# State-space convolution plus gated MLP on one core: squared lag powers on ScalarE, shared first statistics, a new order of work

## The chip, the cores and the metric

The kernel runs on one core of a Trainium2 chip. The core has a matrix engine (TensorE, PE), a vector engine (VectorE, DVE), an engine for activation functions that can also copy, scale and square (ScalarE, ACT), a general engine (GpSimd, POOL), and an engine that issues most of the DMAs (SyncE, SP). Each engine works through its own list of instructions strictly in order; semaphores hold an instruction back until its inputs are there. The metric is the device time of one execution in microseconds (us), lower is better. The kernel before takes 250.21 us, the median of six runs between 249.08 and 250.87 us.

## The reference

One input, `A_u` (2048 positions, 512 channels, bf16), is normalised over its channels and goes through two branches; their sum and the input itself are the output.

```python
def _layernorm(x, axis=-1, eps=1e-5):
    m = jnp.mean(x, axis=axis, keepdims=True)
    v = jnp.var(x, axis=axis, keepdims=True)
    return (x - m) / jnp.sqrt(v + eps)

# branch A: a long convolution whose kernel is a sum of 128 complex modes per channel
dt = exp(log_dt);  logdA = dt * A;  dB = dt * B
P = exp(logdA[:, :, None] * l)                  # powers for l = 0 .. 2047
K = einsum("dn,dnl,dn->dl", C, P, dB).real      # 512 x 2048 kernel
y = irfft(rfft(xn padded) * rfft(K padded))[:L] + xn * Dskip

# branch B: a gated MLP, 512 -> 1792 -> 512
h = sigmoid(xn @ w_gate) * (xn @ w_up)
out = x + y + h @ w_down
```

## The kernel before, in words

**Branch B** is cut into four groups of 512 positions and 14 slices of 128 hidden columns: 56 units. A unit is a gate product on PE (line 977), a sigmoid on ACT (line 986), an up product on PE (line 992) and a product of the two on DVE (line 1007). The up product lies in PSUM. For the units listed in `UEV`, ACT first copies it to `us_sb` in SBUF (line 1003) and DVE reads it there; for the others DVE reads PSUM directly. The units are numbered 14 times the group plus the slice. Four down products per group follow (line 1025).

**Layer norm.** For each of the 16 tiles of 128 positions DVE takes statistics (`bn_stats` and `bn_aggr`, lines 529 and 530) into `mv` (mean and variance). `ln_small` makes the inverse deviation from them: for the first four tiles with small DVE steps (lines 483 to 492) and one power on GpSimd (line 491), for the others with GpSimd, ACT and DVE. The normalised first four tiles are transposed on PE (line 552) and copied out by ACT (line 557); only then can the first gate product start. The others are transposed by DMA.

**Branch A** has these steps.

- A ladder of eleven squarings makes the powers 1, 2, 4, ... 2048 of each mode's complex factor in fp32 (ACT line 650 squares, DVE lines 656 and 658 finish, ACT line 644 casts to bf16 into `W`).
- The powers for all lags are split in two factors. For each of four blocks of 128 channels (c0 to c3) a table `G` of 16 powers and a table `H` of 41 powers are built. `LAG0` lists the lag of each row of `H`. Eight rows of `H` are plain copies of ladder powers (ACT, line 751), row 0 is one, and 32 rows are complex products of an earlier row with a ladder power. `cmul` makes up to 8 such rows at once with four DVE instructions: two of 256 elements per row (lines 710 and 711, `f_a`), and two of 128 elements per row that combine the halves (lines 715 and 716, `f_b`). A complex number lies as two real and two imaginary values side by side.
- PE contracts `G` and `H` over the modes (line 774, 64 matmuls twice per block), ACT copies out (780), PE rearranges (796), ACT copies out (803). `H` is one buffer: the next block's rows wait for these matmuls.
- The spectra: the input transform runs on PE (673) with ACT copies (675) and a trip through DRAM. For each half of the channels (p0, p1) and eight frequency groups (u0 to u7) come PE (847), ACT (852), DMAs, the kernel spectrum on PE (865) and ACT (867), the product on DVE (871 and 875), PE (888), ACT (892) and a store. p0 needs blocks c0 and c1, p1 needs c2 and c3. Final matmuls (945, 947) and adds on DVE (960, 1042) close the work.

**The order** is written out by hand. `_Plan.add` numbers every piece of work as it is added, and the list `ORDER` gives the sequence in which all pieces are issued; each engine's list is that sequence with the other engines' entries left out. The planner's costs (the numbers in `pl.add`) do not act at run time. Entries 0 to 24 are loads; entry 25 is 14 matmuls on zeros whose result is not used (`keep_warm`, line 515), and 26 to 28 are two such matmuls each.

Of the kernel before, what the change touches and what calls it, by code (L numbers as in the profile page):

```python
# [20 lines left out]
D = 512  # L21
# [152 lines left out]
def _consts():  # L174
# [30 lines left out]
UEV = (2, 3, 7, 8, 11, 14, 16, 17, 18, 19, 20, 21, 22, 23, 24, 25, 26, 27, 28, 29, 30, 31, 32, 33, 34, 35, 36, 37, 38, 39, 40, 41, 44, 54, 55)  # L205
ORDER = [
    0, 30, 1, 4, 39, 29, 32, 31, 33, 49, 2, 3, 40, 41, 51, 34, 11, 12, 7, 6, 5, 53, 43, 50, 10, 14, 52, 35, 36, 37, 42, 44,
    54, 45, 46, 47, 22, 15, 38, 56, 48, 27, 614, 55, 615, 138, 28, 616, 59, 637, 95, 96, 141, 677, 60, 638, 678, 93, 682,
    61, 683, 9, 17, 139, 626, 19, 620, 106, 108, 627, 628, 109, 94, 16, 8, 62, 64, 120, 57, 13, 642, 621, 622, 63, 643, 667,
    659, 657, 20, 23, 18, 97, 142, 668, 672, 658, 98, 660, 662, 132, 632, 65, 673, 66, 633, 663, 634, 635, 623, 684, 58, 99,  # L210
    624, 67, 119, 685, 661, 68, 669, 102, 69, 121, 625, 686, 670, 671, 70, 647, 664, 101, 100, 181, 648, 665, 617, 666, 107,
    71, 103, 618, 619, 652, 639, 26, 649, 73, 122, 653, 72, 124, 640, 75, 111, 650, 123, 74, 641, 182, 183, 184, 651, 636,
    76, 629, 674, 135, 644, 675, 645, 24, 140, 143, 104, 125, 133, 224, 630, 225, 77, 226, 676, 79, 185, 679, 654, 25, 136,
    105, 78, 80, 646, 227, 228, 81, 655, 680, 82, 656, 147, 681, 631, 134, 129, 186, 705, 710, 83, 85, 110, 148, 84, 706,
    86, 177, 687, 150, 688, 229, 187, 88, 137, 708, 703, 87, 151, 149, 689, 89, 704, 188, 753, 152, 709, 178, 91, 740, 153,
    690, 128, 192, 711, 191, 127, 126, 695, 154, 230, 189, 712, 741, 194, 193, 168, 765, 199, 171, 112, 113, 696, 179, 155,
    169, 190, 130, 170, 90, 116, 196, 733, 195, 697, 174, 172, 200, 707, 201, 202, 173, 766, 175, 176, 203, 763, 165, 204,
    754, 734, 205, 206, 209, 210, 207, 114, 197, 713, 714, 758, 723, 156, 166, 764, 208, 724, 738, 213, 131, 167, 157, 759,
    92, 739, 760, 214, 159, 158, 211, 212, 215, 216, 767, 160, 198, 742, 231, 735, 745, 144, 736, 145, 115, 737, 232, 217,
    761, 146, 746, 219, 234, 762, 235, 743, 725, 718, 242, 237, 220, 236, 243, 117, 744, 244, 162, 245, 726, 246, 21, 161,  # L220
    727, 747, 247, 258, 118, 768, 748, 163, 769, 719, 749, 267, 259, 268, 770, 730, 269, 771, 164, 772, 239, 218, 720, 750,
    221, 248, 751, 721, 414, 384, 799, 752, 722, 728, 222, 800, 241, 729, 755, 250, 756, 251, 731, 804, 715, 757, 698, 238,
    716, 270, 271, 415, 223, 831, 732, 717, 805, 385, 354, 773, 416, 774, 249, 252, 240, 386, 801, 233, 699, 253, 420, 418,
    256, 353, 257, 254, 255, 272, 775, 421, 355, 260, 802, 356, 262, 261, 273, 263, 277, 358, 274, 360, 361, 419, 417, 388,
    776, 357, 359, 391, 390, 275, 285, 286, 849, 264, 278, 287, 288, 279, 283, 280, 265, 389, 387, 781, 266, 832, 422, 282,
    782, 423, 281, 829, 783, 392, 301, 289, 302, 830, 850, 393, 777, 290, 424, 425, 803, 291, 293, 394, 376, 362, 369, 691,
    276, 395, 294, 851, 839, 363, 310, 833, 784, 406, 852, 840, 399, 370, 292, 426, 364, 789, 365, 809, 371, 427, 284, 810,
    311, 295, 396, 844, 296, 397, 875, 372, 374, 297, 312, 436, 373, 444, 845, 400, 401, 377, 819, 790, 375, 313, 298, 403,
    407, 846, 378, 379, 299, 300, 380, 314, 408, 876, 847, 848, 445, 366, 820, 446, 405, 398, 428, 404, 367, 791, 824, 303,
    305, 304, 825, 792, 806, 437, 306, 402, 320, 321, 322, 315, 853, 807, 448, 324, 438, 429, 368, 841, 834, 316, 409, 793,  # L230
    328, 447, 451, 430, 880, 842, 323, 835, 431, 410, 329, 330, 808, 452, 411, 453, 449, 843, 331, 332, 459, 450, 466, 412,
    821, 822, 811, 460, 812, 333, 454, 455, 381, 814, 461, 327, 881, 813, 382, 344, 823, 435, 432, 434, 815, 325, 816, 836,
    467, 794, 433, 481, 837, 413, 463, 464, 439, 345, 334, 474, 465, 462, 456, 440, 856, 511, 383, 504, 468, 795, 817, 475,
    826, 335, 818, 338, 838, 469, 476, 827, 326, 457, 480, 828, 470, 854, 441, 442, 857, 855, 317, 858, 339, 877, 307, 505,
    878, 308, 506, 796, 319, 797, 785, 458, 489, 309, 937, 798, 318, 336, 471, 887, 938, 888, 490, 337, 342, 895, 859, 882,
    491, 509, 510, 340, 343, 341, 346, 879, 883, 472, 443, 507, 496, 479, 348, 347, 508, 493, 473, 349, 884, 885, 350, 860,
    477, 494, 478, 492, 495, 351, 352, 610, 604, 598, 861, 862, 482, 483, 945, 512, 484, 513, 485, 867, 497, 498, 486, 487,
# [858 lines left out]
```

## Time and profile before

| what | value |
|---|---|
| median of six runs | 250.21 us (249.08 to 250.87) |
| the profiled execution, its own time | 249.7 us |
| its span (first to last instruction) | 247.9 us |
| PE busy | 221.7 us, 89% |
| DVE busy | 199.5 us, 80% |
| ACT busy | 174.0 us, 70% |
| POOL busy | 15.4 us, 6% |
| first sigmoid starts (line 986) | 16.15 us |
| contraction for c0 / c1 / c2 / c3 starts (line 774) | 81.22 / 108.29 / 139.21 / 172.46 us |
| last compute instruction (line 1042) | 244.66 us, lasting 0.42 us |

The profile comes from one execution; about 1.8 us of its time lie outside its span. The four starts of line 774 cut the execution into stages, and busy time is best read stage by stage: a share over the whole span mixes stretches in which different engines are full. An instruction's duration is also longer than what it takes out of its engine's time, because the next one may start before it ends; so where a price is wanted, the distance from one start to the next is read.

### The profile page before, as it was taken

Reading aid. Unit: us, or ns where it says so; the run is one execution under the profiler, and the core shown is the slowest. Engines: PE = TensorE matmul, PEld = TensorE weight load, DVE = VectorE, ACT = ScalarE, POOL = GpSimd, SP = SyncE. Lnnn points to the kernel's source line nnn. Section 1 sums busy time; section 2 is a strip of 40 time slices with the busy share of each in tenths; the row PEclk is TensorE's granted clock in tenths of the full one; section 3 lists DMA queues with packets and bytes.
Section 4 is the critical chain, followed back from the end, with each engine's and each line's share of the span. In section 5 each row is a group of like instructions: output and inputs, shape, how many; then the busy total and the mean of one; then the engine's idle time right before and its main releaser. Section 6 shows DMA issues by size and latency. Waiting matters only on the chain.

```text
span 247.9 us, 5737 instructions
## 1 busy us (share of the span) xinstructions
PE 221.7 (89%) x2246; PEld 119.6 (48%) x2276; DVE 199.5 (80%) x413; ACT 174.0 (70%) x279; POOL 15.4 (6%) x34
## 2 busy tenths in 40 slices
PE   0199899999989998999899999998999998899993
PEld 0155334444433643455455655444665564445761
DVE  3999899999999999999999999999153244673472
ACT  3599999999999987547497899783447897530000
POOL 2202005000000000103000010000010001000000
PEclk9999999999999999999999999999999999999999
DMA  6999933511437472727835786747668479777333
GB/s 151 235 313 379 351 100 106 148 42 59 155 114 182 135 210 85 187 82 169 204 109 151 197 227 165 211 118 197 187 179 262 119 209 260 194 218 248 127 130 127
DMA packets 50861, 43.64 MB, mean 176 GB/s; under 512 B 12561, under 2 KB 44050, under 8 KB 50834
## 3 DMA queue, kind: packets, MB, share of 16 engines
q1 hardware_dynamic: 48738, 40.58, 55.8%
q0 software_dynamic: 864, 1.57, 4.0%
q10 hardware_dynamic: 1232, 1.11, 1.5%
q8 instruction: 18, 0.29, 0.5%
q14 instruction: 9, 0.07, 0.1%
HBM read 24.64 MB, written 12.06 MB: 148 GB/s over the span
## 4 chain that ended last, share of the span: by engine, by line
DVE 48%; PE 31%; ACT 6%; DMA 5%; SPq 5%; issue 3%; DVEq 0%; ACTq 0%
PE bank L1025 11%; DVE big L710 9%; DVE big L711 9%; DVE hT_sb L1007 6%; DVE big L715 5%; DVE big L716 5%; PE bank L977 5%; SPq L412 5%; PE pair L865 4%; DMA big<-c_E 3%; DVE big L871 3%; PE bank L992 2%; DVE big L658 2%; PE pair L945 2%; DVE stats L529 2%
## 5 line engine op out<-in xcount | busy, mean ns | idle before, releaser
L977 PE MATMUL bank<-xnT,wg_sb 128*128 128x512 bf16 (+1 forms) x225 | 55.3, 373 | 4.3 <-ACT hT_sb L986 1.7
L992 PE MATMUL bank<-xnT,wu_sb 128*128 128x512 bf16 x214 | 53.6, 379 | 1.8 <-DVE hT_sb L1007 0.5
L1025 PE MATMUL bank<-wd_sb,hT_sb 128*128 128x512 bf16 x216 | 50.4, 379 | 0.4
L871 DVE TENSOR_TENSOR big<-big 128x2048 bf16<-128x2048 bf16 x16 | 19.5, 1218 | 20.7 <-ACT big L867 19.8
L977 PEld LDWEIGHTS <-wg_sb 128*128 128x128 bf16 x236 | 22.3, 99 | 28.4 <-issue 7.8
L986 ACT ACTIVATE hT_sb<-bank 128x512 bf16<-128x512 f32 x56 | 33.5, 624 | 3.0 <-PE bank L977 3.0
L992 PEld LDWEIGHTS <-wu_sb 128*128 128x128 bf16 x224 | 20.9, 97 | 27.4 <-issue 5.3
L710 DVE TENSOR_TENSOR big<-big 128x256 bf16<-128x256 bf16 (+5 forms) x52 | 33.0, 635 | 1.0
L1025 PEld LDWEIGHTS <-hT_sb 128*128 128x128 bf16 x224 | 21.5, 98 | 25.1 <-DVE hT_sb L1007 0.4
L711 DVE TENSOR_TENSOR big<-big 128x256 bf16<-128x256 bf16 (+5 forms) x52 | 32.9, 633 | 0.0
L1003 ACT ACTIVATE us_sb<-bank 128x512 bf16<-128x512 f32 x35 | 21.1, 606 | 4.1 <-DVE hT_sb L1007 2.5
L867 ACT ACTIVATE big<-pair 128x1024 bf16<-128x1024 f32 x16 | 16.4, 1028 | 9.9 <-PE pair L865 8.9
L715 DVE TENSOR_TENSOR big<-big 128x128 bf16<-128x128 bf16 (+5 forms) x52 | 21.9, 422 | 1.0
L716 DVE TENSOR_TENSOR big<-big 128x128 bf16<-128x128 bf16 (+5 forms) x52 | 21.6, 415 | 0.0
L852 ACT ACTIVATE big<-pair 128x1024 bf16<-128x1024 f32 x16 | 16.6, 1035 | 6.1 <-PE pair L847 6.1
L865 PE MATMUL pair<-big 128*128 128x256 bf16 x160 | 19.6, 273 | 0.7 <-DMA big<-c_E 0.7
L892 ACT ACTIVATE big<-pair 128x1024 bf16<-128x1024 f32 x16 | 16.3, 1030 | 3.2 <-DMA v_scr<-big 2.1
L865 PEld LDWEIGHTS <-big 128*128 128x128 bf16 x160 | 15.4, 98 | 5.5 <-DMA big<-c_E 1.2
L675 ACT ACTIVATE big<-pair 128x1024 bf16<-128x1024 f32 x16 | 17.1, 1067 | 0.0
L1007 DVE TENSOR_TENSOR hT_sb<-hT_sb,bank 128x512 bf16<-128x512 bf16 x21 | 13.9, 678 | 2.4 <-PE bank L992 1.5
L888 PE MATMUL pair<-big 64*64 64x256 bf16 x384 | 13.7, 272 | 1.1 <-DVE big L871 1.1
L1007 DVE TENSOR_TENSOR hT_sb<-hT_sb,us_sb 128x512 bf16<-128x512 bf16 x35 | 14.1, 415 | 0.0
(95 smaller groups left out, 252.4 us busy)
## 6 DMA issues: line engine op xcount, KB each, us to landing
big<-c_E SPq DMA_DIRECT2D x16, 320.0 KB, 3.5
z_scr<-big SPq DMA_DIRECT2D x16, 256.0 KB, 2.5
big<-z_scr SPq DMA_DIRECT2D x16, 256.0 KB, 3.4
big<-big SPq DMA_DIRECT2D x64, 64.0 KB, 3.0
v_scr<-big SPq DMA_DIRECT2D x16, 256.0 KB, 3.1
big<-v_scr SPq DMA_DIRECT2D x12, 256.0 KB, 4.5
big<-in_A_u_dram SPq DMA_DIRECT2D x4, 512.0 KB, 5.2
wu_sb<-in_B_w_up_dram SPq DMA_DIRECT2D x2, 896.0 KB, 9.4
```

The source lines that it names most:

```text
L710: V.tensor_tensor(out=wide(outp), in0=lov, in1=mre, op=ALU.mult)
L711: V.tensor_tensor(out=wide(tb()), in0=lov, in1=mim, op=ALU.mult)
L715: V.tensor_tensor(out=outp[:, :, :, 0, :], in0=outp[:, :, :, 0, :], in1=tb()[:, :, :, 1, :], op=opr)
L716: V.tensor_tensor(out=outp[:, :, :, 1, :], in0=outp[:, :, :, 1, :], in1=tb()[:, :, :, 0, :], op=opi)
L865: T.matmul(two(sk)[:, o:o + DW], es()[:, g, kt, :], kT[p][:, kt, :], start=kt in (0, NKT - 1), stop=kt >= NKT - 2)
L871: V.tensor_tensor(out=pp().rearrange("p q h m -> p (q h) m"), in0=xx().rearrange("p q h m -> p (q h) m"), in1=kb()[:, 0:2 * DW].unsqueeze( ...
L977: T.matmul(bank(sl)[:, c0:c1], w[:, kt, k * 128:(k + 1) * 128], xnT[:, grp, kt, c0:c1], start=(kt == 0), stop=(kt == KT - 1))
L986: S.activation(out=hT_sb[:, hs.idx, k % 2, :], in_=bank(sl), func=ACT.Sigmoid)
L992: T.matmul(bank(sl), wu_sb[:, kt, k * 128:(k + 1) * 128], xnT[:, grp, kt, :], start=(kt == 0), stop=(kt == KT - 1))
L1003: S.activation(out=us_sb[:, us.idx, :], in_=bank(sl), func=ACT.Identity)
L1007: V.tensor_tensor(out=h(), in0=h(), in1=us_sb[:, us.idx, :] if on else bank(sl), op=ALU.mult)
L1025: T.matmul(bank(po), hT_sb[:, hts[k // 2].idx, k % 2, jj * 128:(jj + 1) * 128], wd_sb[:, k, :], start=(k == 0), stop=k == FT - 1, **kw)
```

## The change

- **Lag rows by squaring.** In each of the four `H` tables nine rows (6; 10, 12, 14; 25 to 27; 36 and 38) are now the squares of other rows. ACT squares all parts of the source into the destination in one instruction; DVE then subtracts the imaginary squares from the real ones, multiplies real by imaginary, and doubles that, which are three instructions of 128 elements per row. The other 23 rows are still made by `cmul`, some with a stride in the output, in eight calls where there were nine.
- **First statistics.** For tiles 1 and 3 ACT makes the mean (an identity with `accum_out`) and the mean of squares (a square with `accum_out`). Two small DVE steps per tile turn these into a variance.
- **`UEV`** goes from 35 units to 29: ten leave (2, 3, 8, 11, 20, 22, 23, 27, 44, 55), four come in (15, 42, 46, 49).
- **`ORDER`** is a new list. The numbers are not comparable beyond 180, since each table adds 49 entries and not 43. Entry 25 (the 14 matmuls on zeros) stood in the middle of the first group's up products; it now stands ahead of the first transposes. Nothing else about the computation changes.

```diff
-UEV = (2, 3, 7, 8, 11, 14, 16, 17, 18, 19, 20, 21, 22, 23, 24, 25, 26, 27, 28, 29, 30, 31, 32, 33, 34, 35, 36, 37, 38, 39, 40, 41, 44, 54, 55)
+UEV = (7, 14, 15, 16, 17, 18, 19, 21, 24, 25, 26, 28, 29, 30, 31, 32, 33, 34, 35, 36, 37, 38, 39, 40, 41, 42, 46, 49, 54)
+ON_ACT = (1, 3)
 ORDER = [
-    0, 30, 1, 4, 39, 29, 32, 31, 33, 49, 2, 3, 40, 41, 51, 34, 11, 12, 7, 6, 5, 53, 43, 50, 10, 14, 52, 35, 36, 37, 42, 44,
...
-    76, 629, 674, 135, 644, 675, 645, 24, 140, 143, 104, 125, 133, 224, 630, 225, 77, 226, 676, 79, 185, 679, 654, 25, 136,
...
+    0, 1, 29, 12, 4, 3, 30, 31, 39, 40, 2, 14, 19, 5, 10, 33, 32, 42, 34, 7, 17, 35, 41, 49, 50, 51, 43, 132, 25, 52, 15,
+    36, 44, 133, 53, 134, 8, 11, 45, 46, 37, 47, 27, 54, 94, 96, 38, 48, 644, 638, 645, 55, 639, 106, 6, 640, 646, 119, 650,
...
         if t1 <= LN_ACT:
             def fv_():
+                for i in range(t0, t1):
+                    if i in ON_ACT:
+                        V.scalar_tensor_tensor(out=stats[:, i, 0:1], in0=mv[:, i, 0:1], scalar=-1.0, in1=mv[:, i, 0:1], op0=ALU.mult,
+                                               op1=ALU.mult)
+                        V.tensor_tensor(out=mv[:, i, 1:2], in0=mv[:, i, 1:2], in1=stats[:, i, 0:1], op=ALU.add)
                 V.tensor_copy(out=q["v_b"], in_=mv[:, s, 1])
...
         for i in range(i0, i1):
+            if i in ON_ACT:
+                def fn(i=i):
+                    S.activation(out=glu_sb[:, 7, :], in_=xn[:, i, :], func=ACT.Identity, scale=1.0 / D, accum_out=mv[:, i, 0:1])
+                    S.activation(out=glu_sb[:, 7, :], in_=xn[:, i, :], func=ACT.Square, scale=float(D ** -0.5), accum_out=mv[:, i, 1:2])
+                st.append(pl.add("ACT", 1.42, fn, l_x[i], prio, alt=(56 + i, 3)))
+                continue
...
-                (3, 1, 1, 1, 1, [1]), (5, 1, 1, 3, 2, [1, 2, "3"]), (9, 1, 1, 7, 3, [1, 2, 4, "3", "5"]),
-                (17, 2, 2, 7, 8, [2, 4, 8, "5", "9"]), (25, 4, 4, 3, 9, [4, 8, "9"]), (28, 16, 2, 4, 9, [16, "17"]),
-                (34, 16, 4, 4, 10, [16, 24, "17", "28"]), (38, 26, 4, 2, 10, ["25", "28"]), (33, 8, 1, 1, 10, [8])):
...
+        def squares(o0, os, l0, nn, need):
+            src, dst = H[:, :, l0:l0 + nn, :, :], H[:, :, o0:o0 + (nn - 1) * os + 1:os, :, :]
+            a = pl.add("ACT", 0.11 + 0.213 * nn, lambda: S.activation(out=dst.rearrange("p r k c h -> p r k (c h)"),
+                                                                             in_=src.rearrange("p r k c h -> p r k (c h)"), func=ACT.Square),
+                       dep(need) + hdep, PC - 0.5)
+
+            def f_q():
+                V.tensor_tensor(out=dst[:, :, :, 0, :], in0=dst[:, :, :, 0, :], in1=dst[:, :, :, 1, :], op=ALU.subtract)
+                V.tensor_tensor(out=dst[:, :, :, 1, :], in0=src[:, :, :, 0, :], in1=src[:, :, :, 1, :], op=ALU.mult)
+                V.tensor_scalar(out=dst[:, :, :, 1, :], in0=dst[:, :, :, 1, :], scalar1=2.0, scalar2=None, op0=ALU.mult)
+            h_ops[str(o0)] = pl.add("DVE", 0.18 + 0.185 * nn, f_q, [a], PC - 0.5)
+
+        powers(3, 1, 1, 1, 1, 1, [1])
+        squares(6, 1, 3, 1, ["3"])
+        powers(5, 2, 1, 2, 2, 2, [1, "3"])
+        powers(9, 2, 1, 2, 4, 3, [1, "3", "5"])
+        squares(10, 2, 5, 3, ["5", "6"])
+        powers(17, 1, 2, 2, 7, 8, [2, 4, 8, "6", "10"])
+        squares(25, 1, 17, 3, ["17"])
+        powers(28, 1, 16, 2, 4, 9, [16, "17"])
+        powers(34, 1, 16, 4, 2, 10, [16, "17"])
+        squares(36, 2, 28, 2, ["28"])
+        powers(37, 2, 28, 2, 2, 10, ["28"])
+        powers(33, 1, 8, 1, 1, 10, [8])
```

## The prediction

> **What bounds the kernel now.** I read busy time first, then the slices, then stages, then the order lists. The first part of the page, and from its second part the slices (tenths of 6.2 us each):
>
> ```profile
> PE 221.7 (89%) x2246; PEld 119.6 (48%) x2276; DVE 199.5 (80%) x413; ACT 174.0 (70%) x279; POOL 15.4 (6%) x34
> ...
> PE   0199899999989998999899999998999998899993
> ...
> DVE  3999899999999999999999999999153244673472
> ACT  3599999999999987547497899783447897530000
> ```
>
> DVE is full up to slice 27 and then loose; ACT is full early only; PE is nearly full throughout, since the gated MLP fills it. So the 80% of DVE is two stages: a full one and a loose one. Cut at the first sigmoid and the four contractions (line 774), busy time by stage (time, length, PE, weight loads, DVE, ACT):
>
> ```profile
> 0.00:16.15 16.15, 4.66 (x27) 3.22 (x28) 11.94 (x33) 8.70 (x11) 3.24 (x11) 1.00 0.81 220
> 16.15:81.22 65.07, 61.15 (x279) 27.52 (x284) 63.04 (x140) 64.31 (x110) 5.64 (x11) 1.00 0.54 168
> 81.22:108.29 27.07, 25.57 (x310) 12.56 (x312) 26.48 (x61) 19.61 (x37) 1.43 (x3) 1.00 0.55 155
> 108.29:139.00 30.71, 28.91 (x413) 17.29 (x414) 30.29 (x61) 22.68 (x38) 2.13 (x4) 1.00 0.62 153
> 139.00:172.46 33.46, 32.40 (x469) 17.81 (x473) 33.22 (x68) 26.70 (x43) 1.23 (x3) 1.00 0.69 184
> 172.46:247.90 75.44, 68.98 (x760) 41.16 (x770) 34.50 (x55) 32.04 (x42) 1.73 (x2) 1.00 0.64 187
> ```
>
> From 16.15 to 172.46 (156.3 us) DVE idles 3.3 us in all (156.31 - 153.03), PE 8.3, ACT 23.0, of which ACT's first stage has only 0.8. DVE sets when c3's table is ready; its matmuls even wait for it ("PE pair L774 <- DVE big L715", 0.5 us). After 172.46 PE sets the end. A DVE saving is thus worth something before 172.46 and nothing after; a PE saving is worth something throughout, as far as DVE lets it.
>
> Not all PE work is needed. PE's sequence around 45 us shows the matmuls on zeros in the full stage:
>
> ```profile
> 45.27 3.19 PE L515 MATMUL bank<-glu_sb 128*128 128x512 bf16 x13
> ```
>
> **Prices.** DVE's sequence (start, duration) and rows by shape:
>
> ```profile
> 64.20 0.55 DVE L710 TENSOR_TENSOR big<-big 128x768 bf16<-128x768 bf16 x1
> 64.67 0.55 DVE L711 TENSOR_TENSOR big<-big 128x768 bf16<-128x768 bf16 x1
> 65.25 0.39 DVE L715 TENSOR_TENSOR big<-big 128x384 bf16<-128x384 bf16 x1
> 65.55 0.38 DVE L716 TENSOR_TENSOR big<-big 128x384 bf16<-128x384 bf16 x1
> ...
> L1007 DVE TENSOR_TENSOR hT_sb<-hT_sb,us_sb 128x512 bf16<-128x512 bf16 x35 | 14.1, 415 | 0.0
> L1007 DVE TENSOR_TENSOR hT_sb<-hT_sb,bank 128x512 bf16<-128x512 bf16 x21 | 13.9, 678 | 2.4 <-PE bank L992 1.5 <-ACT big L852 0.8
> ...
> L751 ACT ACTIVATE big<-big 128x256 bf16<-128x256 bf16 x32 | 13.4, 462 | 0.0
> ```
>
> Independent instructions start before the previous one ends (0.47 us apart at 768 elements); one that reads the previous result starts after its end (0.58). Over all sizes in that sequence a start-to-start distance is about 0.066 + 0.134 per row for line 710 (256 elements a row) and 0.085 + 0.067 per row for line 715 (128 a row).
>
> **Lag rows.** A `cmul` of n rows takes 2 x (0.066 + 0.134n) + 2 x (0.085 + 0.067n) = 0.30 + 0.40n of DVE. Per table: before nine calls, 32 rows, 15.6 us; after eight calls, 23 rows, 11.7 us; removed 3.9. Added are four squarings (1, 3, 3, 2 rows): a subtract at line 715's distance (0.18, 0.21, 0.30 for 1, 2, 3 rows), a multiply that the doubling waits for (0.13 more), and the doubling. No row has this doubling (one bf16 source, 128 elements a row); bounds: 0.07, the distance between tiny independent steps (6.43 to 6.50 us, lines 488 and 483), and the 0.27 to 0.39 of a whole line-715 instruction. I take 0.13 to 0.24, nearer to the same shape in line 715. That gives 0.62, 0.72 and twice 0.92: 3.2 per table. With everything at the floor and no wait it is 2.3, with whole durations end to end 4.1. So DVE gets 3.9 - 3.2 = 0.7 to 0.8 per table, 3.0 for four, between 6.6 saved and 0.7 lost.
>
> ACT pays: line 751's 256 elements take 0.31 from start to start in a row of three, line 644's 512 elements 0.52; I take 0.38, 0.58, 0.79 for 1, 2, 3 rows, 2.5 per table, 10.1 in all.
>
> The Trainium skill, "VectorE: DVE Perf Modes", section "The perf-mode tier table", gives a bf16 `tensor_scalar` in SBUF four times the base rate and `tensor_tensor` twice. By it the doubling would be the cheapest of the three steps, towards the floor; no row here shows it on pairs of two values. The same skill, "ScalarE: Activation LUTs", section "Rules for kernel authors", says to leave multiplies to VectorE, up to about three times faster per element in bf16. That speaks against the change, and the rows agree in direction: 256 elements cost 0.20 on DVE (line 710) and 0.31 on ACT. By that rule alone the sum of both engines' work only grows; by the stages the work leaves the engine that is full for one with idle time from 81 us on.
>
> **Products.** Six units more read PSUM: 0.60 instead of 0.335 from start to start, +1.6 on DVE; ACT loses six copies of 0.48, 2.9.
>
> **Statistics.** DVE loses two pairs of 0.79 (lines 529, 530) and gains four dependent tiny steps of 0.21: -0.7. ACT gets four passes over 512 elements, 2.4 by line 593's 0.66 and line 609's 0.52 spacing (the accumulator is in no row; bounds 2.1 and 3.8 with a tiny 0.2 step after each and no overlap), while it idles 3.3 us waiting for `log_dt`.
>
> **Order.** I priced every entry of both lists this way and summed between landmarks (us of work, before / after):
>
> | from, to | PE | DVE | ACT |
> |---|---|---|---|
> | start, first sigmoid | 3.8 / 7.2 | 12.2 / 12.5 | 7.4 / 10.8 |
> | to contraction c0 | 58.7 / 60.9 | 66.3 / 64.3 | 65.4 / 63.8 |
> | to c1 | 24.7 / 22.1 | 21.8 / 21.7 | 16.3 / 19.7 |
> | to c2 | 28.6 / 26.5 | 29.7 / 29.8 | 23.2 / 25.2 |
> | to c3 | 31.5 / 30.7 | 31.8 / 31.8 | 24.3 / 27.2 |
> | to the end | 67.8 / 67.8 | 32.4 / 31.8 | 31.0 / 30.5 |
>
> Up to c3 DVE has 1.7 less (161.8 to 160.1), 0.6 of the 2.3 falling after it, where it buys nothing. Between first sigmoid and c3 PE has 3.4 less (143.5 to 140.2), because 3.0 us of zeros now run while PE idles before the first transposes, and ACT 6.7 more.
>
> The head gets later. DVE must wait for ACT's statistics of tile 1 (landing 3.69, two passes to 4.95, where DVE is done at 4.5), then four tiny steps where there were two; stepping through the new order, line 603 ends at 11.5, not 11.0, so sines, copies (557) and first sigmoid come 0.5 later, and DVE reaches the ladder 0.7 behind. SP's new order lets the first gate weights land later too (issued about 6.6, not 4.7; landing took 3.8), still ahead of 14.
>
> **Sum.** DVE -1.7, head +0.7, and part of the 3.3 us in which DVE idles goes with PE further ahead (lines 1007's wait for up products, 1.5 in all; I take 0.5, bounds 0 and 1.5): -1.5 up to c3. The tail has the same PE work: 0. The profiled execution, 249.7 (247.9 span and 1.8 around it), would become 248.2; it stands 0.5 below the median of 250.21, so I predict 248.7.
>
> **Rivals.**
> - *DVE stalls at the hand-offs* (slower). Sixteen squarings go DVE to ACT to DVE; all queued DVE work stands behind one that waits, and PE's contraction behind that. The new order puts 1.3 to 9.1 us of DVE work between producer and finish. Tightest are c1's row 6 (1.78, against 1.28 + 0.38 on ACT) and c1's rows 36 and 38 (1.31 against 0.50 + 0.58). ACT is full up to 81 us and may be behind. Against: the ladder's eleven hand-offs of this kind (650 to 658) have no line in the waits. It decides from 1.5/16 = 0.09 us each; at 0.25 each, 4.0 - 1.5 = 2.5 slower: 252.7.
> - *Squares at the floor* (faster). 3.6 us more off DVE; PE would need 148.0 - 3.4 = 144.6 busy of 151.2, about as full as now, so I give it half: 246.9.
> - *No change.* The two handed-back terms (products 1.6, head 0.7) and a full ACT eat the gain, as PE's tail is untouched: 250.2.
>
> **Chances.** Forecast (247.4 to 249.8) 0.42, floor 0.16, no change 0.20, stalls 0.22. 0.5% of 250.2 is 1.25 us, about what can be told here. Three quarters of the forecast's chance and all of the floor's lie under 248.95: faster 0.48; the rest of the forecast and most of no change, 0.26, same; slower 0.26. Leaving a tenth out at each side: 246.0 to 252.5; the forecast alone 247.4 to 249.8.
>
> **What would show it.** Right: c3's contraction near 171.2, the first sigmoid near 16.7, no matmuls on zeros after 25 us, three DVE steps after each square totalling 0.6 to 0.95, ACT 85 to 90% full between. Wrong: waits of DVE on the new ACT square (rival one), the three steps under 0.5 for one row (rival two), or a tail longer than 75.4 because the last spectra come later.

## The result and the profile after

| | before | after |
|---|---|---|
| median | 249.53 us (36 runs) | 252.56 us (17 runs, 251.10 to 254.76) |
| ratio | 1 | 1.0119, 95% interval 1.0096 to 1.0142 |
| profiled execution | 249.7 us, span 247.9 | 252.05 us, span 250.3 |
| first sigmoid | 16.15 | 16.54 |
| contraction c0 / c1 / c2 / c3 | 81.22 / 108.29 / 139.21 / 172.46 | 83.86 / 111.36 / 140.58 / 175.96 |

The kernel became 1.2% slower; 248.7 us had been forecast. The page of after, busy time and slices (6.3 us each):

```profile
PE 222.0 (89%) x2246; PEld 119.5 (48%) x2276; DVE 202.0 (81%) x445; ACT 184.2 (74%) x297; POOL 15.5 (6%) x34
...
PE   0799999999987799599999799979699999999994
...
DVE  2999999999999999999999999999335244662652
ACT  5799999999998988457998699877446589740000
```

The picture of before stands: DVE is full for 27 slices, then loose. It has 2.5 us more to do, not less. The same, by stage, cut at the first sigmoid and the four contractions (time, length, PE, weight loads, DVE, ACT, POOL, granted clock, DMA share, GB/s):

```profile
0.00:16.54 16.54, 8.47 (x54) 4.99 (x55) 11.53 (x37) 12.32 (x19) 3.23 (x11) 1.00 0.84 245
16.54:83.86 67.32, 61.84 (x279) 27.48 (x283) 65.67 (x149) 66.10 (x114) 6.82 (x12) 1.00 0.52 154
83.86:111.36 27.50, 24.44 (x296) 11.76 (x298) 26.78 (x68) 19.02 (x35) 0.35 (x2) 0.94 0.52 146
111.36:140.58 29.22, 26.95 (x403) 16.45 (x405) 28.67 (x63) 26.18 (x42) 0.36 (x2) 1.00 0.61 173
140.58:175.96 35.38, 31.66 (x464) 17.65 (x470) 34.80 (x78) 27.73 (x45) 3.03 (x5) 1.00 0.65 165
175.96:250.30 74.34, 68.61 (x759) 41.20 (x770) 34.55 (x57) 32.83 (x43) 1.73 (x2) 0.99 0.67 192
```

From first sigmoid to c3 DVE is busy 155.92 of 159.42 us (153.03 of 156.31 before), so it idles 3.5 us, as before, and the stretch is 3.1 longer because DVE's work is 2.9 longer. The head adds 0.4, and the tail gives 1.1 back (74.34 for 75.44): together the 2.4 by which the span grew. The granted clock, 0.94 in one stage of after and 1.00 in all of before, is not the cause: the four runs of after whose mean clock was 1.000 took 253.29 to 254.03 us, the four at 0.986 251.36 to 254.54.

Where DVE's time went, as the distance from each start to the next (an instruction's own duration where DVE stood idle behind it), first sigmoid to c3:

| work | before | after | difference |
|---|---|---|---|
| table products (before 710, 711, 715, 716; after 729, 730, 734, 735) | 95.5 | 81.8 | -13.7 |
| steps of the squares (789, 790, 791) | 0 | 15.7 | +15.7 |
| unit products (1007; 1051) | 16.6 | 18.6 | +2.0 |
| statistics (529, 530; 547, 548) | 8.6 | 6.2 | -2.4 |
| phases ahead of the ladder (595; 613) | 3.3 | 4.5 | +1.2 |

The last two rows are in part work that moved across the first sigmoid: one tile of statistics more falls ahead of it, two phase steps more behind it. The lag rows did not save 3.0 us, they cost 2.0 (15.7 - 13.7), and waits between the squares' steps come on top (0.6 ahead of 790 and 0.5 ahead of 791; other waits became shorter by about as much, since DVE idles 3.5 us in all and 3.3 before):

```profile
L790 DVE TENSOR_TENSOR big<-big 128x384 bf16<-128x384 bf16 (+2 forms) x16 | 6.3, 394 | 0.6
L789 DVE TENSOR_TENSOR big<-big 128x384 bf16<-128x384 bf16 (+2 forms) x16 | 6.2, 387 | 0.0
L791 DVE TENSOR_SCALAR big<-big 128x384 bf16<-128x384 bf16 (+2 forms) x15 | 4.3, 285 | 0.5
```

DVE's sequence in table c0 shows why (start, duration):

```profile
67.19 0.27 DVE L789 TENSOR_TENSOR big<-big 128x128 bf16<-128x128 bf16 x1
67.49 0.28 DVE L790 TENSOR_TENSOR big<-big 128x128 bf16<-128x128 bf16 x1
67.80 0.23 DVE L791 TENSOR_SCALAR big<-big 128x128 bf16<-128x128 bf16 x1
67.94 0.63 DVE L734 TENSOR_TENSOR big<-big 128x512 bf16<-128x512 bf16 x1
68.48 0.62 DVE L735 TENSOR_TENSOR big<-big 128x512 bf16<-128x512 bf16 x1
...
70.48 0.50 DVE L789 TENSOR_TENSOR big<-big 128x384 bf16<-128x384 bf16 x1
71.02 0.51 DVE L790 TENSOR_TENSOR big<-big 128x384 bf16<-128x384 bf16 x1
71.56 0.34 DVE L791 TENSOR_SCALAR big<-big 128x384 bf16<-128x384 bf16 x1
72.01 1.09 DVE L729 TENSOR_TENSOR big<-big 128x1792 bf16<-128x1792 bf16 x1
```

Two things are to be seen. First, the subtract, the multiply and the doubling each start only after the one before has ended: the multiply overwrites the imaginary squares that the subtract reads, and the doubling reads the multiply's result. One row costs 0.75 us (67.19 to 67.94), three rows two apart 1.53 (1.34 to 1.55 in the four tables). Second, rows two apart slow the combining steps: line 734 at 512 elements takes 0.54 here from start to start; further on in the same profile, with adjacent rows, 0.35. The other two groups, 25 to 27 and 36, 38, take 1.06 and 1.03. The four sum to 4.4 us in this table (4.2 to 4.4 in the four), above even the ceiling of 4.1.

### The profile page after: what moved, and what is told of

Same layout as the page of the kernel before. It is cut to its first block, busy times and chain, and to the rows that moved or that the text cites. A ratio compares the mean times of both kernels' runs of the same rounds, so it can differ in the third digit from the quotient of the medians.

```text
span 250.3 us, 5787 instructions
## 1 busy us (share of the span) xinstructions
PE 222.0 (89%) x2246; PEld 119.5 (48%) x2276; DVE 202.0 (81%) x445; ACT 184.2 (74%) x297; POOL 15.5 (6%) x34
## 4 chain that ended last, share of the span: by engine, by line
DVE 43%; PE 23%; ACT 21%; issue 6%; DMA 4%; SPq 2%; DVEq 0%; ACTq 0%
DVE big L729 8%; DVE big L730 8%; PE bank L1069 7%; DVE big L735 6%; DVE big L734 5%; ACT big L662 4%; PE pair L909 4%; DVE hT_sb L1051 4%; PE bank L1036 4%; DVE big L915 3%; ACT hT_sb L1030 3%; PE bank L1021 3%; ACT big L693 3%; ACT big L668 3%; PE pair L932 2%
## 5 line engine op out<-in xcount | busy, mean ns | idle before, releaser
L1036 PE MATMUL bank<-xnT,wu_sb 128*128 128x512 bf16 x214 | 54.3, 379 | 3.2 <-DVE hT_sb L1051 1.2
L1069 PE MATMUL bank<-wd_sb,hT_sb 128*128 128x512 bf16 x217 | 52.0, 388 | 1.0 <-ACT glu_sb L1099 0.5
L1030 ACT ACTIVATE hT_sb<-bank 128x512 bf16<-128x512 f32 x56 | 32.3, 599 | 4.0 <-PE bank L1021 4.0
L729 DVE TENSOR_TENSOR big<-big 128x512 bf16<-128x512 bf16 (+4 forms) x48 | 27.7, 577 | 1.0 <-ACT big L770 0.2
L730 DVE TENSOR_TENSOR big<-big 128x512 bf16<-128x512 bf16 (+4 forms) x48 | 27.5, 573 | 0.0
L1051 DVE TENSOR_TENSOR hT_sb<-hT_sb,bank 128x512 bf16<-128x512 bf16 x27 | 17.8, 681 | 7.2 <-ACT hT_sb L1030 4.6
L1047 ACT ACTIVATE us_sb<-bank 128x512 bf16<-128x512 f32 x29 | 17.1, 603 | 6.8 <-DVE hT_sb L1051 6.1
L734 DVE TENSOR_TENSOR big<-big 128x256 bf16<-128x256 bf16 (+4 forms) x48 | 20.2, 420 | 0.8
L735 DVE TENSOR_TENSOR big<-big 128x256 bf16<-128x256 bf16 (+4 forms) x48 | 19.9, 414 | 0.0
L911 ACT ACTIVATE big<-pair 128x1024 bf16<-128x1024 f32 x16 | 16.5, 1032 | 4.4 <-PE pair L909 3.2
L896 ACT ACTIVATE big<-pair 128x1024 bf16<-128x1024 f32 x16 | 16.3, 1032 | 3.3 <-PE pair L891 3.3
L936 ACT ACTIVATE big<-pair 128x1024 bf16<-128x1024 f32 x16 | 16.3, 1026 | 1.8 <-DMA v_scr<-big 1.1
L693 ACT ACTIVATE big<-pair 128x1024 bf16<-128x1024 f32 x16 | 16.3, 1025 | 1.6 <-PE pair L691 1.6
L691 PE MATMUL pair<-big,s 128*128 128x512 bf16 x31 | 9.7, 394 | 7.9 <-DVE big L559 7.8
L784 ACT ACTIVATE big<-big 128x768 bf16<-128x768 bf16 (+2 forms) x16 | 11.1, 691 | 6.2 <-DVE big L735 6.1
```

What stands on the lines that cost most here:

```text
L693: ev = pl.add("ACT", 0.90, lambda sl=sl, zs=zs: S.activation(out=zs().rearrange("p j d -> p (j d)"), in_=two(sl), func=ACT.Identity), [fx_ ...
L729: V.tensor_tensor(out=ov, in0=lov, in1=mre, op=ALU.mult)
L730: V.tensor_tensor(out=wide(tb()), in0=lov, in1=mim, op=ALU.mult)
L734: V.tensor_tensor(out=outp[:, :, :, 0, :], in0=outp[:, :, :, 0, :], in1=tb()[:, :, :, 1, :], op=opr)
L735: V.tensor_tensor(out=outp[:, :, :, 1, :], in0=outp[:, :, :, 1, :], in1=tb()[:, :, :, 0, :], op=opi)
L1030: S.activation(out=hT_sb[:, hs.idx, k % 2, :], in_=bank(sl), func=ACT.Sigmoid)
```

## The experiments

Each time stands beside the kernel before on the same chip (249.3 to 249.5 us); "repaired order" means that the list is kept, but an entry whose inputs do not exist yet is issued at the first place where they do (so in all kernels but e3, e4, e5, e17, e19, e21 and e22). "Below after" is the distance from after's 252.56 us, which comes from other runs; the median of before beside those (249.53 us) differs from those here by at most 0.24 us.

### Making the row work cheaper where it stands

Rows side by side in four of the five strided calls (rows 5 and 7 stay two apart; some rows then hold other lags), repaired order:

```diff
-        powers(9, 2, 1, 2, 4, 3, [1, "3", "5"])
-        squares(10, 2, 5, 3, ["5", "6"])
+        powers(9, 1, 1, 2, 4, 3, [1, "3", "5"])
+        squares(13, 1, 5, 3, ["5", "6"])
...
-        squares(36, 2, 28, 2, ["28"])
-        powers(37, 2, 28, 2, 2, 10, ["28"])
+        squares(36, 1, 28, 2, ["28"])
+        powers(38, 1, 28, 2, 2, 10, ["28"])
```

> The changed kernel with the stride of two rows taken out of the destinations of four calls per table (the rows 9, 11, 13, 15 now lie at 9 to 12, rows 10, 12, 14 at 13 to 15, rows 36 to 39 likewise); the same instructions on as many elements, but rows 9 to 15 and 36 to 39 then hold other lags than the output needs, so the output is not the reference's. Theory A with the stride as a part of the price: line 734 took 0.54 us from start to start at 512 elements in strided rows and 0.345 in adjacent ones, the squares of three rows 1.5 against 1.06; that is about 1.1 us per table, 4 us in all on VectorE, and the time falls by 2 to 4 us. If the stride costs nothing on the path, or by theory B: less than 1 us.

Measured: 249.99 us, 2.6 below after; DVE busy 198.2 (202.0). The same place in the sequence, DVE of this kernel:

```profile
67.92 0.44 DVE L743 TENSOR_TENSOR big<-big 128x512 bf16<-128x512 bf16 x1
68.27 0.45 DVE L744 TENSOR_TENSOR big<-big 128x512 bf16<-128x512 bf16 x1
...
70.10 0.39 DVE L798 TENSOR_TENSOR big<-big 128x384 bf16<-128x384 bf16 x1
70.52 0.39 DVE L799 TENSOR_TENSOR big<-big 128x384 bf16<-128x384 bf16 x1
70.94 0.29 DVE L800 TENSOR_SCALAR big<-big 128x384 bf16<-128x384 bf16 x1
```

The first pair starts 0.35 apart where it took 0.54; the three steps take 0.39, 0.39, 0.29 for 0.50, 0.51, 0.34. The stride is a cost of its own, as theory A had it. By the sums of the table above, the products take 79.9 us in this kernel (81.8 in after) and the steps of the squares 13.9 (15.7): with adjacent rows the lag rows take 1.8 less of DVE's time than in before, not 2.0 more.

The doubling left out:

```diff
                 V.tensor_tensor(out=dst[:, :, :, 1, :], in0=src[:, :, :, 0, :], in1=src[:, :, :, 1, :], op=ALU.mult)
-                V.tensor_scalar(out=dst[:, :, :, 1, :], in0=dst[:, :, :, 1, :], scalar1=2.0, scalar2=None, op0=ALU.mult)
```

> The changed kernel without the last of the three VectorE steps after each square (the doubling); the imaginary parts of nine rows are then half of what they should be, and the output is not the reference's. Theory A: sixteen steps and the waits in front of them go, about 1.3 us per table by the distances in the profile (0.27, 0.3, 0.3 and 0.5), 5 us in all on VectorE; the time falls by 3 to 5 us. Theory B: VectorE is not what sets the time, less than 1.5 us.

Measured: 248.44 us, 4.1 below after; DVE busy 197.4. A step of 0.23 to 0.36 us cost 0.26 each, within theory A.

Both edits together:

> The kernel after with both edits of e2 and e3: the destinations of the strided groups moved side by side (some rows then hold other lags) and the doubling left out. Issue order unchanged. Theory A (in the kernel after DVE's work for the rows passes into the time one to one, since DVE is full from the first sigmoid to c3): the two savings of 2.6 and 4.1 us add, 245.3 to 247.0 us. Theory B (another engine becomes the bound after the first few us): 247.8 or more.

Measured: 245.37 us (ratio 0.9828, 0.9793 to 0.9864), 7.2 below after; the two single gains sum to 6.7. Its page and stages up to c3:

```profile
PE 220.7 (91%) x2246; PEld 119.3 (49%) x2276; DVE 194.4 (80%) x429; ACT 183.8 (75%) x297; POOL 15.5 (6%) x34
```

```profile
16.70:81.96 65.26, 61.89 (x279) 27.54 (x283) 63.62 (x145) 65.03 (x114) 6.85 (x12) 1.00 0.53 159
81.96:106.57 24.61, 22.75 (x297) 11.46 (x299) 24.02 (x62) 19.57 (x36) 0.35 (x2) 1.00 0.53 154
106.57:134.61 28.04, 26.90 (x404) 16.46 (x405) 27.59 (x61) 24.90 (x41) 0.35 (x2) 1.00 0.64 173
134.61:169.71 35.10, 31.86 (x464) 17.72 (x470) 33.18 (x75) 28.98 (x47) 3.02 (x5) 1.00 0.70 179
```

DVE's 7.6 us became 7.2 us of time (6.5 between the two profiled spans), and c3 comes 6.2 earlier. The forecast's mechanism held: what is taken off DVE ahead of c3 is gained nearly in full here, and less fully in e2 (3.8 us of busy time for 2.6). Only the sign of what the rows did to DVE was wrong.

### The same work added to before

Rows 10, 12, 14 and 25 to 27 of each table get one more DVE step (times 1.0), order untouched:

```diff
+            if more is not None:
+                V.tensor_scalar(out=more[:, :, :, 1, :], in0=more[:, :, :, 1, :], scalar1=1.0, scalar2=None, op0=ALU.mult)
```

> The kernel before with its own order and rows, and one more DVE step behind two of the nine products of each table: rows 10, 12, 14 and rows 25 to 27 are multiplied by 1.0 (imaginary halves), an instruction of the form of the doubling. Nothing is left out. Priced from the trace of after at 0.45 (strided) and 0.32 us per table, 3.1 in all, about what DVE has more to do in after than in before. Theory A (DVE's work alone explains the result): 251.6 to 253.2 us, the time of after. Theory B (DVE has cover in before that the new order took away): 250.6 or less.

Measured: 252.01 us, ratio 1.0120 (1.0069 to 1.0170), the ratio of the change itself. DVE of this kernel in table c0:

```profile
68.55 0.61 DVE L716 TENSOR_TENSOR big<-big 128x896 bf16<-128x896 bf16 x1
69.19 0.35 DVE L718 TENSOR_SCALAR big<-big 128x384 bf16<-128x384 bf16 x1
69.58 1.09 DVE L710 TENSOR_TENSOR big<-big 128x1792 bf16<-128x1792 bf16 x1
```

DVE busy is 201.9 (199.5), the time 2.6 higher. (The profile is of the longest of the four runs, 254.81 us; up to c3, at 175.35, it is 2.9 later than before, and its tail is 2.2 longer.) So 2.4 to 2.9 us of DVE work ahead of c3 suffice to explain a result of this size without a new order.

An estimate of what is left for the order, from e16 and after: there 7.6 us of DVE were worth 7.2 us of time, so at before's 199.5 us of DVE the new order would stand at 250.2, 0.7 above before. Single kernels lie 1.0 (e2) and more off that line, so the 0.7 is not shown to be more than scatter.

### The other parts, alone, in before

`UEV` and the new order were not tried alone.

The matmuls on zeros (entry 25) moved ahead of the first transposes:

```diff
-... 5, 53, 43, 50, 10, 14, 52, 35, 36, 37, ...   -... 679, 654, 25, 136, ...
+... 5, 53, 43, 50, 10, 14, 52, 35, 25, 36, 37, ...   +... 679, 654, 136, ...
```

> The kernel before with one entry moved: the 14 matmuls on zeros run ahead of the first transposes and not at 45 us. The prediction gave PE's relief 0.5 us (0 to 1.5), as VectorE sets the pace up to 172 us: 0 to 0.6% faster. If PE's 3.0 us were worth their length: 1.0 to 1.2% faster. If the filler only stood where PE had to wait anyway: no change.

Measured: 249.64 us, ratio 1.0018 (0.9999 to 1.0036). PE's relief is worth nothing in before: the 0.5 us of the forecast is gone.

The statistics of tiles 1 and 3 on ScalarE, with the code of after:

> The kernel before with one edit: the statistics of tiles 1 and 3 on ScalarE, as in the kernel after; order, lag rows and UEV untouched. Theory A (what the change lost it lost in the price of the lag rows): nothing to be told from before, 248.8 to 249.9 us, since 0.7 us of DVE is saved and the DVE's wait for ScalarE's sums gives about as much back ahead of the first sigmoid. Theory B (a later start is what makes the change slower): at least 1.2 us above before, 250.5 or more, with the first sigmoid at 16.6 or later.

Measured: 249.11 us, ratio 0.9996 (0.9965 to 1.0027). No difference, to within 0.9 us.

### Cheaper squares in place

The multiply and the doubling in one instruction per row:

```diff
-                V.tensor_tensor(out=dst[:, :, :, 1, :], in0=src[:, :, :, 0, :], in1=src[:, :, :, 1, :], op=ALU.mult)
-                V.tensor_scalar(out=dst[:, :, :, 1, :], in0=dst[:, :, :, 1, :], scalar1=2.0, scalar2=None, op0=ALU.mult)
+                for k in range(nn):
+                    V.scalar_tensor_tensor(out=dst[:, :, k, 1, :], in0=src[:, :, k, 0, :], scalar=2.0, in1=src[:, :, k, 1, :],
+                                           op0=ALU.mult, op1=ALU.mult)
```

> The kernel after, all computed, with the multiply and the doubling of a square put into one instruction per row (two times real, times imaginary). Order unchanged. From the rows: 0.2 to 0.25 us per row instead of about 0.3 to 0.54 for the multiply and 0.27 to 0.45 for the doubling of a whole group, 0.9 us less per table. Theory A: 3 to 4 us under after, 248.6 to 249.8, no slower than before. Theory B (nine instructions instead of eight, and one that runs at a lower rate, cost as much): 251.5 or more.

Measured: 251.34 us, 1.2 below after and between the two theories; DVE busy 200.2. The four squares take 0.52, 1.34, 1.04 and 0.83 us (3.7 for 4.4), so 0.6 per table were saved and half of the 2.6 arrived. Its profile has the first sigmoid at 17.5, not 16.5, and from there to c3 (175.56) it takes 158.1 us, 1.3 less than after; more on the head below.

The doubling of rows 25 to 27 on GpSimd for c0 to c2 (only the contraction reads them), the rest as in e19, and rows 36 to 39 side by side:

```diff
+                if on_pool:
+                    V.tensor_tensor(out=dst[:, :, :, 1, :], in0=src[:, :, :, 0, :], in1=src[:, :, :, 1, :], op=ALU.mult)
+                    return
...
+                h_ops[str(o0)] = pl.behind(q, "POOL", lambda: P.tensor_scalar(out=dst[:, :, :, 1, :], in0=dst[:, :, :, 1, :], scalar1=2.0,
+                                                                              scalar2=None, op0=ALU.mult))
```

> The kernel after, all computed, with the squares made cheaper for DVE in place: for tables c0 to c2 the doubling of rows 25 to 27 is done by GpSimd (only the contraction reads these rows), the other squares take the doubling into the multiply as in e19, and lags 1544 and 1792 change places so that rows 36 to 39 are written side by side. Order of DVE, PE and ScalarE unchanged. From the rows: 0.3 (25 to 27), 0.2 (6), 0.2 (10, 12, 14), 0.35 (36, 37), 0.15 (38, 39), 1.2 us of DVE less per table. Theory A (DVE's row work passes into the time): 2.5 to 4.8 us under after, 247.8 to 250.1. Theory B (as in e19, half of it is lost to other waits): 250.2 to 251.

Measured: 250.53 us, ratio 1.0031 (1.0008 to 1.0054), in theory B's range. GpSimd takes 1.20 to 1.32 us for what takes DVE 0.28. With rows 36 and 37 there too:

> As e21, with the doubling of rows 36 and 37 on GpSimd too for c0 to c2; these rows are made shortly ahead of the contraction. Theory A: 0.2 us of DVE less per table than e21, 247.2 to 249.8. Theory B (GpSimd's doubling is slow and the contraction waits for it): later than e21, 250 or more, with PE's contraction waiting for GpSimd.

Measured: 250.98 us, ratio 1.0040 (1.0002 to 1.0078), theory B; the contraction waits 1.0 us for GpSimd in all, twice. Of the kernels that leave nothing out, none came out measurably under before.

### The three steps not behind one another

`f_q` cut into three pieces of work, other DVE work between them:

```diff
-            h_ops[str(o0)] = pl.add("DVE", 0.18 + 0.185 * nn, f_q, [a], PC - 0.5)
+            q1 = pl.add("DVE", 0, lambda: ..., [a])
+            q2 = pl.later("DVE", q1, lambda: ...)
+            h_ops[str(o0)] = pl.later("DVE", q2, lambda: ...)
```

> The kernel after with the same instructions and the same rows, but the three steps of each square (subtract, multiply, doubling) no longer directly behind one another: the multiply is issued one piece of other DVE work later, the doubling one piece later again. Nothing is left out. Theory A (most of what the squares cost above their price is that each step stands until the one before it has ended): 2 to 3.5 us below after, 249.0 to 250.6, with the steps starting 0.3 rather than 0.43 (three adjacent rows) after the instruction before them. Theory B (what costs is the number and shape of the steps, not their waits): at most 0.6 below after, 252 or more.

Measured: 259.89 us. DVE of this kernel shows a mistake of placing, not an answer:

```profile
128.68 0.50 DVE L808 TENSOR_TENSOR big<-big 128x384 bf16<-128x384 bf16 x1
134.41 1.23 DVE L934 TENSOR_TENSOR big<-big 128x2048 bf16<-128x2048 bf16 x1 [5.23 <-PE pair L951]
135.55 0.33 DVE L810 TENSOR_SCALAR big<-big 128x384 bf16<-128x384 bf16 x1
```

The doubling (L810) had been put behind a spectrum product that waits for PE, and the next rows with it. In the same way with rows relaid side by side:

> A kernel that computes everything: as e8_square_steps_apart, and the lags are laid out in other rows of the table, so that every row group that is written or combined is adjacent (odd lags 1 to 15 in rows 1 to 8, then 8, 12, 4, 2, 6, 10, 14; 256, 264, 268, 260, 258, 262, 266, 270; and so on). Rows for lags 6, 10, 14 are one square of three rows, lag 12 is a product of one row; nine products and three squares per table. Theory A (waits and strides are separate costs that add up): 2 to 3 us below e8, 246.3 to 248.5, faster than before by 0.4 to 1.2%. Theory B (DVE would no longer be what sets the end after the first of the two savings): 248.8 or more, with DVE idle up to the last contraction well over the 3.5 us of after.

Measured: 259.08 us, with the same kind of loss between c1 and c2 (110.56 to 149.65 us). Then with steps apart only behind table work:

> As e8_square_steps_apart, whose DVE list had a doubling behind a spectrum product that waits for PE (5.2 us of DVE standing at 128.7 us, with c2's rows queued behind it). Now a step goes one piece later only where that piece is a product for a table or a lag row; elsewhere the three steps stay together. The lists of PE, ScalarE and POOL are those of the kernel after. 11 of the 16 squares or so get at least one step apart. Theory A (each step stands until the one before it has ended): 1 to 2.5 us below after, 250.1 to 251.6. Theory B (the waits between the steps are worth nothing): 252 or more.

Measured: 252.38 us (ratio 1.0130, 1.0104 to 1.0157), 0.2 below after; DVE busy 201.1, 0.9 less. By the time, theory B's bound is met. By the profile, first sigmoid (17.4) to c3 (175.41) takes 158.0 us, 1.4 less than in after, and the later head takes most of it back. The waits were removed for a part of the squares only; that they are worth anything in time is not shown. Side by side and apart:

> As e10_rows_side_by_side_steps_apart (all computed; every group of rows adjacent, lag 12 by a product), with the steps apart by the rule of e11. Theory A (strides and waits add up, and DVE sets the end up to the last contraction): 2 to 3 us below e11, 247.3 to 249.3, with DVE's busy time 5 us under that of after. Theory B (another engine takes over): 250.5 or more, with DVE idle where after had it full.

Measured: 251.24 us, ratio 1.0084 (1.0061 to 1.0107); DVE busy 198.6, 3.4 less than after, for 1.3 us. Together with the multiply that doubles, and no step moved apart:

> As e19, all computed, with the lag rows laid out as in e12 (every group that is written is adjacent; nine products, three squares per table) and no step moved apart. Theory A: 2 to 3 us under e19, 246.3 to 248.3, faster than before. Theory B (as e12 showed, a list with other dependencies meets new waits): 249 to 251, with DVE idle in the stages where after had it full.

Measured: 251.00 us, DVE busy 199.0. Both laid the rows out so that other rows depend on each other than the order was made for. They miss theory A by 1.9 and 2.7 us and lie where theory B put them. In part DVE's gain went into idling: 6.1 us from first sigmoid to c3 in e12 and 6.3 in e20, where after has 3.5; why DVE idles there was not settled.

### Rows moved between the two kernels

Four kernels put the rows of one kernel into the order of the other: nine products in after (e1, and e7 with the copies of ladder powers early), four squares in before (e14), one square in before (rows 25 to 27, e15).

```diff
-        squares(25, 1, 17, 3, ["17"])
+        powers(25, 1, 4, 4, 3, 9, [4, 8, "9"], True)
...
```

> The changed kernel, its order, units and statistics kept, but the nine squared rows and their neighbours are made by complex products again, in the nine calls of the kernel before; ScalarE's sixteen squares are gone. Theory A (the rows cost VectorE more than the products they replace: in the profiles the products took 109.5 us and products plus squares 111.8, and the contraction of c3 came 3.5 us later): VectorE gets 2 to 4 us back before that contraction, and the time falls by 2 to 4 us, to within 0.5% of the kernel before or below it. Theory B (the new order is bad, or ScalarE too full): ScalarE gets 11 us back, PE's order is the same, and the time stays 0.8% or more above the kernel before.

Measured: 261.29 us. DVE waits 6.2 us for ScalarE's copies of ladder powers (0.2 in after), which the products need earlier than the squares did.

> The kernel after with the nine products of before for the lag rows (no squares), as in e1_rows_by_product, but with ScalarE's eight copies of ladder powers into a table issued together at the place of the first of them, so that the products find theirs done. Order of everything else, UEV and statistics as after. Theory A (the squares and the strided rows cost more than the products they replace): DVE's busy time 2 to 3 us under that of the kernel after, and a time of 249 to 251 us, below the 252.6 of after. Theory B (the new order with the later head is slow by itself): 252 or more, with DVE still waiting or PE starved though the copies are early.

Measured: 254.08 us, DVE busy 200.9: theory A missed, theory B's bound met. DVE idles 5.8 us from first sigmoid to c3 (3.5 in after), and the sigmoid itself comes at 17.3. Whether that is the new order by itself, or that it was made for other rows, these runs don't separate.

> The kernel before with the lag rows of the kernel after (eight products and four squares per table, strides as there) put into before's own order: each square on ScalarE behind the row that it needs, each set of three steps behind the product that stood there. Head, statistics, UEV and PE's list are those of before. Theory A (the price of the lag rows is the cause by itself): DVE's busy time up by 2 to 3 us, 251.5 to 253.5 us, about the time of after. Theory B (the new order, its head and UEV are the cause): 249 to 250.3, no worse than before.

Measured: 281.79 us. The waits of this kernel:

```profile
ACT big L778 <- DVE big L730: 16.6, 6, 5.9
```

```profile
DVE big L783 <- ACT big L778: 12.8, 5, 5.8
```

ScalarE's square (L778) stands in its queue until DVE has its source, with sigmoids queued behind it, and DVE's subtract (L783) waits for the square in turn. This is the forecast's first rival, and here it is real. In after only ScalarE's square waits for DVE (6.1 us, four times, line 784); DVE's subtract (line 789) never stands for the square.

> The kernel before with one of its products replaced in each table: rows 25 to 27, three adjacent rows, are the squares of rows 17 to 19 (ScalarE squares, DVE subtracts, multiplies and doubles as in the kernel after, 1.06 us against 1.5 for the product). No row has a stride. Theory A (a square pays where its rows are adjacent and three or more): 0.4 us less DVE per table, 247.6 to 249.2 us. Theory B (a square costs more than its DVE steps, by ScalarE's time or a hand-off): 249.8 or more, with DVE waiting for the square.

Measured: 251.01 us, ratio 1.0054 (1.0029 to 1.0080), as theory B had it, though DVE's busy time fell by 2.2 us to 197.3. DVE now waits 1.5 for one square (it is late on a ScalarE that waited 2.7 for a down product) and 0.9 for a copied up product; up to c3 it idles 6.8 us, 3.5 more than before. So the saving in DVE's work is real, and new waits take more than it gave.

The times of these four don't say what the row work costs by itself, because an order written out by hand fits one set of dependencies. The edits in place (e2, e3, e16, e17) do. The traces do too, by the sums of the table above: products alone take 95.5 us in before's order and 96.3 and 96.5 in after's (e1, e7), products and squares 97.5 in after's and 97.9 in before's (e14). The squares with strided rows are the dearer kind in either order, by 1.0 to 2.3 us.

## Why the prediction was wrong

**What bounds the kernel: right.** DVE sets the end up to c3. e16 and e17 show it in both kernels, in both directions, at close to one to one.

**Lag rows: the step that failed, and with it the sign.** "Removed 3.9, added 3.2" per table was 3.4 and 3.9 (the table above, divided by four), plus 0.3 of waits between steps. Instead of 3.0 us saved, 2.0 lost and 1.1 of waits. Of this error of 5.0, the stride is 3.8 (e2's sums); the squares' steps above their price make most of the rest. With the term so corrected and the tail's 1.1 gained, the forecast's -1.5 becomes the 2.4 by which the span grew; the errors of the other terms cancel.
- The squares' three steps were priced as if only the doubling waited. The multiply waits too, since it writes where the subtract reads, and the step after an end starts 0.03 to 0.04 later, not overlapped (16 of 16 in after). One row was priced 0.62 and took 0.75; three rows 0.92, against 1.06 adjacent and 1.53 strided; two rows 0.72, against 1.03 in rows two apart.
- "cmul, some with a stride" was priced as adjacent. At 512 elements line 734 takes 0.54 for 0.35; lines 729 and 730 are not slowed (0.61 at 1024 elements). e2 puts the stride of four of the five strided calls at 2.6 us of time.
- The bounds 6.6 saved to 0.7 lost came from rows of adjacent data only, so the true value lay outside them.

**Products: right.** +1.6 was forecast for six units; +2.0 was measured up to c3, with seven more of the 42 units there read from PSUM.

**Statistics: right in size.** A tile costs 0.8 on DVE (8.6 us for 11), the four small steps 0.8 together, and e5 finds no difference from the whole edit. The accumulator, in no row before, takes 0.19 behind a pass of 0.63; ScalarE's four passes took 2.9 (3.80 to 6.69), forecast 2.4.

**Relief of PE: wrong.** The 0.5 is nothing (e4), and DVE idles no less in after.

**Head: right in size in the profiled run, and it isn't one number.** "3.0 us of zeros now run while PE idles before the first transposes" was costed at nothing. PE and ScalarE of after, and of e22, whose head is the same code, and ScalarE of before:

```profile
8.64 4.17 PE L526 MATMUL bank<-glu_sb 128*128 128x512 bf16 x14
12.64 1.06 PE L570 MATMUL pair<-ident,big 128*128 128x128 bf16 x16
13.31 1.92 ACT L575 ACTIVATE xnT<-pair 128x1024 bf16<-128x1024 bf16 x2
```

```profile
8.63 5.74 PE L534 MATMUL bank<-glu_sb 128*128 128x512 bf16 x14
14.21 1.06 PE L578 MATMUL pair<-ident,big 128*128 128x128 bf16 x16
14.85 1.94 ACT L583 ACTIVATE xnT<-pair 128x1024 bf16<-128x1024 bf16 x2 [1.45 <-PE pair L578]
```

```profile
12.62 1.99 ACT L557 ACTIVATE xnT<-pair 128x1024 bf16<-128x1024 bf16 x2
```

The zeros stand behind two spectrum matmuls that wait until 7.8 us for the first normalised tile, and take 0.30 to 0.41 us each, where they took 0.25 in the middle of before (13 in 3.19). The last normalised tile is ready at 12.4 in both; the transposes wait for the zeros until 12.64 or 14.21, and the first sigmoid comes at 16.54 or 18.10. In after's own profile that wait cost nothing: ScalarE is busy without a break from 8.88 us to the first sigmoid, and its own work from there on sets the first copy of a transposed tile, 0.7 later than in before. In e22 ScalarE stands 1.45 us for the transposes. In the profiles of the 14 kernels with this order that wait was 0 to 1.45 us, and the sigmoid came between 16.5 and 18.1; in those with the order of before (before, e4, e5, e14, e15, e17) it came between 16.05 and 16.18, in e5 too, which has the new statistics. In e4 the zeros took as long (5.17) but started at 1.36 and were done in time. The Trainium skill, "TensorE: Matmul & The Clock Gate", section "What's actually happening", says that the array runs at half rate until some 3.4 us of sustained work have passed, and that the number of slow matmuls varies from run to run because the window runs freely. The halving and the variation agree: the distance from one of these matmuls to the next falls from 0.43 to 0.22 us, but 2.9 us after PE's first matmul in after and 5.9 us after it in e22, on both sides of the page's figure. The granted clock in the profile reads 1.00 over these matmuls, so these traces show it by the distances alone. That the zeros' place explains part of the loss, the small gain of e19 and the wider scatter of such kernels (e2's runs spread over 3.0 us, those of before beside it over 1.5) is argued, not shown: no run moved the zeros back in the kernel after.

**Tail:** forecast unchanged, 1.1 us shorter; why is open. **The rivals:** "DVE stalls at the hand-offs" named nearly the measured time (252.7), by luck: its wait isn't in the trace of after. "No change" was right that the products and the head give time back, but not in what the rows cost; none of the rivals had the rows cost more than what they replaced.

**The signs named beforehand:** first sigmoid 16.7 (16.54) and ScalarE 85 to 90% full (87%) came in; matmuls on zeros after 25 us are left at 32.2 (two), where none were forecast. c3 at 171.2 was 175.96, and three of the four sets of three steps left the 0.6 to 0.95 that was named (1.03, 1.06, 1.53). That last line was the one to trust: it points at the term that failed.

## What to carry to other kernels

Price a chain of short steps by whole durations end to end, and look for a write over something that the step before still reads: it costs a wait like a true dependency. Price an access pattern only from a row with the same pattern; rows two apart are not rows side by side. When a full engine hands work to another, count what it gets back in finishing steps first: here the nine rows of a table gave 3.4 us of products away and took 3.9 us of finishing back. And test a suspected cost in place; work moved between two hand-written orders mostly measures the order.

## What the runs showed of the hardware

- Rows of four values two rows apart (so that every other row is skipped) cost `tensor_tensor` on VectorE 0.54 instead of 0.35 us from start to start at 512 elements and 0.30 instead of 0.23 at 256, but only in the steps that take half of each row; those that take whole rows keep their time (0.61 at 1024 elements either way).
- A step that reads what the step before it wrote, or overwrites what that step reads, started 0.03 to 0.04 us after its end; with neither, steps of 384 elements start 0.30 apart at durations of 0.39.
- The doubling (one source) takes 0.225 us for 128 elements and 0.28 for 384 adjacent ones, the subtract 0.275 and 0.385. The slope is about half, as the Trainium skill's "VectorE: DVE Perf Modes", section "The perf-mode tier table", has it for one source against two, but at this size the fixed part is what is paid. The same page's section "The TRN2 errata — SBUF-src ops pay a fixed extra latency per instruction" says that many small tiles pay a fixed latency per tile; the doubling agrees, with 0.06 us more for three times the elements.
- `accum_out` on ScalarE shows as a second instruction of 0.19 us behind each pass.
- GpSimd's doubling of 384 elements took 1.20 to 1.32 us, over four times VectorE's 0.28.
- Fourteen matmuls on zeros took 4.1 to 5.7 us in the profiles of the 14 kernels with one and the same head.
